# Raw expert weights fetched from slot 8 on, transposes one chunk ahead, and the row products in two halves of 64 tokens

## The chip, the cores and the metric

One core of a Trainium2 chip runs the whole program. The metric is the time of one execution on the device in microseconds (us), the median of several runs. Five engines work side by side, each through its own queue in order: TensorE (PE in the profile; its weight loads are PEld), VectorE (DVE), ScalarE (ACT), GpSimd (POOL) and SyncE (SP), which here only issues DMAs.

## What is computed

A linear attention with a decaying state, and behind it a mixture of experts with one expert per token:

```python
def _attn_ref(r, k, v, w, u):             # B, H, S, D = 4, 8, 768, 48
    state = zeros((B, H, D, D))
    for t in range(S):
        y[:, :, t] = r_t @ (state + outer(u * k_t, v_t))
        state = w_t[:, None] * state + outer(k_t, v_t)

def _moe_ref(x, w_skip, w_gate, w1, w2):  # x = y as (3072, 384), E = 8, F = 1024
    do_compute = x @ w_skip > 0           # the others keep x
    e_idx = argmax(xc @ w_gate);  gate_w = softmax(xc @ w_gate) at e_idx
    for e in range(E):
        h = maximum(xc[mask_e] @ w1[e], 0)
        out[mask_e] = xc[mask_e] + gate_w * (h @ w2[e])
```

## The kernel before

**Attention.** The 3072 tokens are 24 chunks of 128 (four sequences of six chunks; chunks 5, 11, 17 and 23 end a sequence). A loop over s (the slots, from -2 to 24) treats three chunks at a time: chunk s+2 is prepared, chunk s+1 gets its scores, and chunk s its outputs. The order of every queue is the order in which this code is written out.

- SP loads chunk s+4 (`load_chunk`: `wrk` with decays, r and k, 578 KB, and `vt` and `vN` with v) and writes the rows of a finished chunk to `out` (`store`, L479). `wrk` has three buffers, `vt` four.
- POOL makes `p` (L330), `rk` (L332) and the odd columns of r (L339) of chunk s+3, behind `kq` of chunk s+2 (L360, in `prep_keys`).
- DVE scans (`prep_scan` L344, L362), scales r to `rp` (L367), masks the scores (`mask` L396, twice a chunk) and multiplies the bonus into psY (`bonus` L408). From slot 12 on it also has the steps of the router (L248), a few of them per slot.
- PE runs per slot: `update` of the state (L418), `outputs` (L444, L450), `scores` (L380), `keys` (L389, four transposes of `kq`, copied by ACT to `kt` at L391 for the next `update`; a chunk that ends a sequence has none), `bonus_sums` (L404), and `rows_out` (L464). `quadratic(i)` at L299 writes out scores, mask, keys, bonus_sums and bonus of one chunk. `rows_out` turns the chunk's output `xT` into rows, with the router's logits beside them: four products with 128 tokens as the weights and 105 moving columns.
- ACT copies results out of the accumulators (L391, L456, L474, L478, L436).

**Experts.** Every expert has two weight matrices; each is fetched raw (3 pieces of 0.5 MB on SP, `load_weights`, L101) and split into a high part (ACT copies it to a rounded type) and a low part (raw minus high): six slices of 512 columns for each matrix. `raws[e, q]` names the raw tile of expert e: q=0 for w1 and q=1 for w2. Raw tile `r0` holds (0,0), `r1` holds (0,1), and then (1,0), and then (1,1), so each of these fetches waits until the one ahead in that tile has been split.

Two tables say when this is done in the attention: `W_AT` (fetch of (0,1) in slot 19, of (0,0) in slot 20, of (1,0) in slot 24) and `S_AT` (slices 6 to 11, that is w2 of expert 0, in slots 21 to 23, high part on ACT and low part on POOL, L710). What is left of expert 1's w1 is split in the passage behind the loop.

**The passage between.** Behind slot 24 the last router group (chunks 18 to 23) runs on DVE, while PE computes expert 0's first 128 tokens (`early_expert`, L137 and L628). Four of the six slices of (1,0) are put into the queues there (`first_split`, L733: ACT, then POOL), then the token list `idr` is made (L748), POOL gathers the second 128 tokens of expert 0 (`gather(1, None)`, L720 into `xg1`), and the last two slices follow. PE transposes these tokens (`early_tokens(1)`, L598), finishes the first ones (last four products of L628; DVE adds `fin0` at L631) and starts on the second ones (L137 again, in `expert(0)`). Then come experts 1 to 7, PE without a gap.

## Time and profile before

| | |
|---|---|
| runs | 313.95, 313.95, 315.13 us; median 313.95 |
| the profiled execution | 313.69 us, of which 311.8 us are the span from the first to the last instruction |
| attention, to the last `rows_out` | to 147.9 us of the span |
| passage to expert 1's tokens | 147.9 to 177.0 us |
| experts behind it | 177.0 to 311.8 us |
| PE busy over the span | 282.8 us (91%) |
| DVE, ACT, POOL busy | 222.8, 135.5, 161.9 us |

Times in the rows are microseconds from the span's start unless marked ns. Where a row has a start and a duration, the durations of matmuls overlap, since they are pipelined; from one group's start to the next one's is what a group costs. In brackets stands the idle time of the engine before a row and whose event ended it.

### The profile page before, as it was taken

The page shows a single profiled execution, that of the slowest core. Times are in us where ns is not written, and L with a number is a line of the kernel's source. Part 1 is how long each engine was busy: PE and PEld are TensorE (multiplying, and loading weights), DVE is VectorE, ACT ScalarE, POOL GpSimd, SP SyncE. Part 2 cuts the span into 40 slices and gives each one's busy share as a digit, 9 for nine tenths or more (in the row PEclk, how much of TensorE's full clock was granted, in tenths as well). Part 3 has the DMA queues.
Part 4 walks back from the last instruction along what each step waited for, and adds up shares of the span by engine and source line. Part 5 has one row for each costly group of instructions (what it writes and reads, how often), then busy time and mean ns, then how long its engine had stood idle before and what let it go on. Part 6 is the DMA issues. An engine that isn't in the chain of part 4 may idle for free.

```text
span 311.8 us, 8950 instructions
## 1 busy us (share of the span) xinstructions
PE 282.8 (91%) x3593; PEld 254.8 (82%) x3593; DVE 222.8 (71%) x481; ACT 135.5 (43%) x336; POOL 161.9 (52%) x155
## 2 busy tenths in 40 slices
PE   7979999999799797979935999999999999999892
PEld 2568878887687676767825999999999999999892
DVE  7789888878899996983840669586776849495320
ACT  3034334433343241335430659292957749182300
POOL 8899999897787787365493412231212223201111
PEclk9999999999999997999995899999999999999999
DMA  6999989869866868821629298969698784820001
GB/s 189 238 238 249 286 247 261 259 170 277 228 173 200 233 190 246 315 97 60 223 80 330 72 355 290 363 220 300 235 318 282 222 302 140 258 103 25 8 6 39
DMA packets 27706, 64.93 MB, mean 208 GB/s; under 512 B 4156, under 2 KB 15392, under 8 KB 27654
## 3 DMA queue, kind: packets, MB, share of 16 engines
q1 hardware_dynamic: 25350, 58.46, 61.1%
q0 software_dynamic: 2048, 5.48, 5.3%
q8 instruction: 30, 0.49, 0.7%
q10 hardware_dynamic: 256, 0.33, 0.4%
q14 instruction: 22, 0.18, 0.2%
HBM read 57.20 MB, written 7.86 MB: 209 GB/s over the span
## 4 chain that ended last, share of the span: by engine, by line
PE 70%; DVE 12%; DMA 8%; POOL 4%; issue 3%; ACT 1%; SPq 1%; POOLq 0%; DVEq 0%; ACTq 0%
PE psO L879 7%; PE psO L877 7%; PE psO L878 7%; PE psH L850 7%; PE psH L852 6%; PE psH L851 6%; PE psY L444 6%; PE psA L380 5%; DVE asb L396 4%; PE psY L450 3%; DMA vt<-wrk 3%; PE psX L464 3%; PE psY L404 3%; DVE psY L408 3%; PE psT L389 3%
## 5 line engine op out<-in xcount | busy, mean ns | idle before, releaser
L814 POOL DMA_INDIRECT out<-fin,ids x16 | 16.9, 1057 | 84.3 <-DVE fin L884 51.4
L850 PE MATMUL psH<-xTh,w1h 128*128 128x256 f32 x168 | 47.6, 284 | 0.0
L852 PE MATMUL psH<-xTh,w1l 128*128 128x256 f32 x168 | 47.5, 283 | 0.0
L851 PE MATMUL psH<-xTl,w1h 128*128 128x256 f32 x168 | 47.5, 283 | 0.0
L857 ACT ACTIVATE hh<-psH 128x256 fp32r<-128x256 f32 x60 | 23.3, 389 | 54.7 <-PE psH L852 47.9
L877 PE MATMUL psO<-w2h,hh 128*128 128x384 f32 x120 | 40.8, 340 | 0.0
L858 DVE SCALAR_TENSOR_TENSOR hl<-psH,hh 128x256 fp32r<-128x256 f32 x60 | 25.3, 421 | 21.7 <-ACT hh L857 21.4
L879 PE MATMUL psO<-w2h,hl 128*128 128x384 f32 x120 | 40.2, 335 | 0.0
L878 PE MATMUL psO<-w2l,hh 128*128 128x384 f32 x120 | 40.1, 334 | 0.0
L360 POOL TENSOR_TENSOR kq<-wrk,q 128x512 f32<-128x512 f32 x24 | 26.9, 1119 | 20.5 <-DVE q L344 13.6
L339 POOL TENSOR_TENSOR wrk<-wrk 128x512 f32<-128x512 f32 x24 | 36.1, 1506 | 2.4 <-DVE rk L332 0.6
L396 DVE TENSOR_TENSOR asb<-psA,c_sb 128x512 f32<-128x512 f32 x48 | 30.8, 684 | 8.1 <-PE psA L380 7.9
L456 ACT COPY xT<-psY 128x512 f32<-128x512 f32 x24 | 14.1, 586 | 48.8 <-PE psY L450 35.5
L852 PEld LDWEIGHTS psH<-xTh,w1l 128*128 128x128 f32 x168 | 32.2, 192 | 0.0
L850 PEld LDWEIGHTS psH<-xTh,w1h 128*128 128x128 f32 x168 | 32.2, 191 | 0.0
L851 PEld LDWEIGHTS psH<-xTl,w1h 128*128 128x128 f32 x168 | 32.2, 192 | 0.0
L444 PE MATMUL psY<-asb,vN 128*64 128x128 f32 (+1 forms) x384 | 26.6, 282 | 4.5 <-DVE psY L408 4.3
L720 POOL DMA_INDIRECT xg<-out,idr x15 | 16.2, 1078 | 27.3 <-PE psH L852 14.0
L332 POOL TENSOR_TENSOR rk<-wrk 128x512 f32<-128x512 f32 x23 | 29.5, 1283 | 0.0
L107 DVE TENSOR_TENSOR w2l<-r,w2h 128x512 fp32r<-128x512 f32 x42 | 27.8, 687 | 0.4
L884 DVE SCALAR_TENSOR_TENSOR fin<-psO,gates,xg 128x384 f32<-128x384 f32 x15 | 9.3, 618 | 25.1 <-PE psO L879 25.1
L107 DVE TENSOR_TENSOR w1l<-r,w1h 128x512 fp32r<-128x512 f32 x36 | 24.8, 689 | 1.8
(155 smaller groups left out, 653.3 us busy)
## 6 DMA issues: line engine op xcount, KB each, us to landing
r<-w SPq DMA_DIRECT2D x48, 512.0 KB, 6.4
wrk<-wrk SPq DMA_DIRECT2D x23, 577.9 KB, 6.0
wp<-wrk SPq DMA_DIRECT2D x9, 516.0 KB, 4.7
vN<-vN SPq DMA_DIRECT2D x12, 384.0 KB, 4.2
out<-x SPq DMA_DIRECT2D x24, 192.0 KB, 4.0
vt<-wrk SPq DMA_DIRECT2D x24, 96.0 KB, 3.9
vt<-wrk SPq DMA_DIRECT2D x48, 48.0 KB, 3.7
out<-fin,ids POOLq DMA_INDIRECT x16, 4.5
```

What stands on the lines that cost most here:

```text
L107: (eng or nc.vector).tensor_tensor(dst_l, src, dst_h.bitcast(F32), op=ALU.subtract)
L332: (nc.gpsimd if i else nc.vector).tensor_tensor(rk.rearrange("p a j -> p (a j)"), t[:, R_OFF:K_OFF], t[:, K_OFF:V_OFF], op=ALU.mult)
L339: nc.gpsimd.tensor_tensor(rk1, rk1, two(1, 1, CW), op=ALU.mult)
L360: nc.gpsimd.tensor_tensor(pairs(kq), pairs(wk["k"]), twice(wk["q"][:, :, 1:HW]), op=ALU.mult)
L396: nc.vector.tensor_tensor(s, psa[g], tri.rearrange("p (o j) -> p o j", o=1).to_broadcast([P, NP, P]), op=ALU.mult)
L444: nc.tensor.matmul(quarter(0, a, g, w), head(i, 2 * a + g, w), wk["asb"][g][:, a], start=False, stop=(c == 0), skip_group_check=True)
L850: nc.tensor.matmul(ps, w1h[:, o:o + P], xTh[:, kc], start=(kc == 0), stop=False)
L851: nc.tensor.matmul(ps, w1h[:, o:o + P], xTl[:, kc], start=False, stop=False)
L852: nc.tensor.matmul(ps, w1l[:, o:o + P], xTh[:, kc], start=False, stop=(kc == KC - 1))
L877: nc.tensor.matmul(pso, h[j, fc][0], w2h[:, o], start=(fc == 0), stop=False)
L878: nc.tensor.matmul(pso, h[j, fc][0], w2l[:, o], start=False, stop=False)
L879: nc.tensor.matmul(pso, h[j, fc][1], w2h[:, o], start=False, stop=(fc == FC - 1))
```

## The change

1. **Raw weights.** `W_AT` now has one piece of 0.5 MB in each of nine slots: (0,1) in slots 8, 10 and 12, (1,0) in 14, 16 and 18, and (0,0) in 19, 20 and 21. (1,0) gets a raw tile of its own, `r2`.
2. **Split.** The high parts of (0,1) and (1,0) are cast on ACT one per slot, in slots 11 to 22, behind `store`. Ten low parts go to POOL in slots 21 to 23, ahead of `evict`, and two to DVE at the end of slots 22 and 23. `S_AT` and `first_split` are gone, and so are the subtractions in the passage.
3. **Transposes.** `keys` is taken out of `quadratic` and called for chunk s+2 behind it; `bonus_sums` follows `scores` at once.
4. **Rows.** `rows_out` makes eight products of 64 tokens each where it made four of 128; the two halves of the tokens go to the two halves of the output's partitions.

```diff
-W_AT = {19: ((0, 1),), 20: ((0, 0),), 24: ((1, 0),)}
-S_AT = {21: ((0, 6), (0, 7)), 22: ((0, 8), (0, 9)), 23: ((0, 10), (0, 11))}
+W_AT = {8: (0, 1), 10: (0, 1), 12: (0, 1), 14: (1, 0), 16: (1, 0), 18: (1, 0), 19: (0, 0), 20: (0, 0),
+        21: (0, 0)}
+CASTS = [(0, i) for i in range(6, 12)] + [(1, i) for i in range(6)]
+CAST0 = 11
+LOWS = {21: CASTS[:3], 22: CASTS[3:7], 23: CASTS[7:10]}
+LOWS_V = {22: CASTS[10:11], 23: CASTS[11:]}
...
     def load_weights(e, q):
-        m = 1 if e == 1 else q
-        wr = wset0.tile([P, KC * DF], F32, tag=f"r{m}", name=f"r{m}_{e}{q}")
+        if (e, q) == (1, 0):
+            wr = third[0]
+        else:
...
+        third.append(pers.tile([P, KC * DF], F32, name="r2"))
...
             mask(i, 1)
-            keys(i)
             bonus_sums(i)
...
             for a in range(NP):
                 o = (a // 2) * X2 + (a % 2) * 2 * D
-                nc.tensor.matmul(px[:, o:o + XW], xT[:, a],
-                                 wgo_sb[:, a // 2] if a % 2 else wgp_sb[:, a], start=(a == 0),
-                                 stop=(a == NP - 1), skip_group_check=True)
+                for j in (0, HP):
+                    nc.tensor.matmul(px[j:j + HP, o:o + XW], xT[:, a, j:j + HP],
+                                     wgo_sb[:, a // 2] if a % 2 else wgp_sb[:, a],
+                                     start=(a == 0), stop=(a == NP - 1), skip_group_check=True)
...
                 if on(s - 1):
                     store(s - 1)
+                if 0 <= s - CAST0 < len(CASTS):
+                    cast(*CASTS[s - CAST0])
...
                         products(s + 3)
+                for i in LOWS.get(s, ()):
+                    low(*i, nc.gpsimd)
                 if on(s):
                     evict(s)
...
                     drip(2 * pace[0])
+                if on(s + 2):
+                    keys(s + 2)
...
+                for i in LOWS_V.get(s, ()):
+                    low(*i, nc.vector)
                 if s in W_AT:
-                    for e, q in W_AT[s]:
-                        drain(load_weights(e, q))
-                for i in S_AT.get(s, ()):
-                    split_slice(*i, nc.gpsimd)
-                    nc.gpsimd.tensor_tensor(*lows.pop(0), op=ALU.subtract)
+                    if W_AT[s] not in gens:
+                        gens[W_AT[s]] = load_weights(*W_AT[s])
+                    next(gens[W_AT[s]])
...
-                if 8 <= turn < 12:
-                    first_split()
...
             gather(1, None)
-            while firsts:
-                first_split()
             drain(load_weights(1, 1))
```

PE's queue in slot 5, from the last score of chunk 6 to the first output of chunk 6 (`psT` are the transposes, `psX` the rows, `psu` the state), before:

```order
L380 MATMUL psA1_113<-rp6_691,kq6_679 64x64
L389 MATMUL psT6_789<-c_sb_94,kq6_679 128x128 x4
L404 MATMUL psY_111<-rk6_592,ubk_sb_95 64x128 x8
L464 MATMUL psX5_805<-wgp_sb_101,xT5_764 128x105
L464 MATMUL psX5_805<-wgo_sb_102,xT5_764 128x105
L464 MATMUL psX5_805<-wgp_sb_101,xT5_764 128x105
L464 MATMUL psX5_805<-wgo_sb_102,xT5_764 128x105
L418 MATMUL psu_110<-vN1_90,kt6_794 64x48 x8
L444 MATMUL psY_111<-asb0_6_785,vN1_90 64x128
```

And after:

```order
L393 MATMUL psA1_114<-rp6_708,kq6_696 64x64
L417 MATMUL psY_112<-rk6_612,ubk_sb_96 64x128 x8
L402 MATMUL psT7_826<-c_sb_95,kq7_784 128x128 x4
L478 MATMUL psX5_833<-wgp_sb_102,xT5_792 64x105 x2
L478 MATMUL psX5_833<-wgo_sb_103,xT5_792 64x105 x2
L478 MATMUL psX5_833<-wgp_sb_102,xT5_792 64x105 x2
L478 MATMUL psX5_833<-wgo_sb_103,xT5_792 64x105 x2
L431 MATMUL psu_111<-vN1_90,kt6_745 64x48 x8
L457 MATMUL psY_112<-asb0_6_813,vN1_90 64x128
```

The bonus sums have moved ahead of the transposes, the transposes are those of chunk 7 instead of chunk 6, and the rows are eight products of 64 tokens.

POOL's queue from its last `kq` to the gathers for expert 1 (`w2l0` and `w1l1` are low parts, `xg` gathered tokens), before:

```order
L360 TENSOR_TENSOR kq23_2320<-wrk2_84,q23_2301 128x512
L587 DMA xg0_64<-out,id0_70 128x384
L710 TENSOR_TENSOR w2l0_0_2378<-r1_01_2165,w2h0_0_2377 128x512 x6
L733 TENSOR_TENSOR w1l1_1_2550<-r1_10_2501,w1h1_1_2549 128x512 x4
L720 DMA xg1_65<-out,idr_2506 128x384
L733 TENSOR_TENSOR w1l1_1_2550<-r1_10_2501,w1h1_1_2549 128x512 x2
L720 DMA xg2_2667<-out,idr_2506 128x384
```

And after:

```order
L373 TENSOR_TENSOR kq23_2429<-wrk2_84,q23_2410 128x512
L132 TENSOR_TENSOR w2l0_0_1317<-r1_01_1121,w2h0_0_1316 128x512 x3
L601 DMA xg0_64<-out,id0_70 128x384
L132 TENSOR_TENSOR w2l0_0_1317<-r1_01_1121,w2h0_0_1316 128x512 x3
L132 TENSOR_TENSOR w1l1_1_1938<-r2_91,w1h1_1_1937 128x512 x4
L740 DMA xg1_65<-out,idr_2616 128x384
L740 DMA xg2_2763<-out,idr_2616 128x384
```

Three subtractions have moved ahead of the first gather, and two of the twelve have left POOL for DVE.

SP's queue from the store of chunk 20 on (`r1_11` is the raw w2 of expert 1), before:

```order
L479 DMA out<-x20_2284 128x384
L479 DMA out<-x21_2384 128x384
L479 DMA out<-x22_2454 128x384
L479 DMA out<-x23_2491 128x384
L101 DMA r1_10_2501<-w12 128x1024 x3
```

And after:

```order
L493 DMA out<-x20_2392 128x384
L108 DMA r0_00_2273<-w12 128x1024
L493 DMA out<-x21_2488 128x384
L108 DMA r1_11_2716<-w12 128x1024 x3
L493 DMA out<-x22_2564 128x384
L493 DMA out<-x23_2605 128x384
```

The fetch of (1,0) behind the stores is gone, and that of (1,1) stands ahead of the last two stores.

## Rows read from the trace of the kernel before

**Rows 1.** The page: granted TensorE clock in 40 slices, in tenths.

```profile
PEclk9999999999999997999995899999999999999999
```

**Rows 2.** Stages: span, length, busy PE PEld DVE ACT POOL, PEclk, DMA share, GB/s.

```profile
55.30:60.50 5.20, 5.20 (x113) 4.42 (x109) 4.26 (x9) 2.04 (x7) 4.48 (x5) 1.00 0.72 192
...
103.50:110.00 6.50, 4.78 (x96) 3.93 (x92) 6.32 (x17) 1.90 (x7) 5.25 (x5) 1.00 0.81 236
...
115.40:124.90 9.50, 7.03 (x119) 6.03 (x115) 6.64 (x20) 2.52 (x9) 7.49 (x9) 0.82 0.84 261
```

**Rows 3.** PE in order of time, a full slot: start, duration, line, operation.

```profile
55.27 0.47 PE L464 MATMUL psX<-wgp_sb,xT 128*128 128x105 f32 x2
...
56.34 0.67 PE L418 MATMUL psu<-vN,kt 128*64 128x48 f32 x16
56.84 1.05 PE L444 MATMUL psY<-asb,vN 128*64 128x128 f32 x16
57.82 0.66 PE L450 MATMUL psY<-rp,sblk 64*64 64x128 f32 x16
58.30 1.05 PE L380 MATMUL psA<-rp,kq 64*64 64x64 f32 x32
59.29 0.66 PE L389 MATMUL psT<-c_sb,kq 128*128 128x128 f32 x4
59.87 0.67 PE L404 MATMUL psY<-rk,ubk_sb 64*64 64x128 f32 x16
60.47 0.36 PE L464 MATMUL psX<-wgp_sb,xT 128*128 128x105 f32 x1
```

**Rows 4.** PE in order of time, the slots around chunk 2 and slot 4.

```profile
22.93 1.05 PE L380 MATMUL psA<-rp,kq 64*64 64x64 f32 x32
...
38.58 1.05 PE L380 MATMUL psA<-rp,kq 64*64 64x64 f32 x32
39.47 0.67 PE L404 MATMUL psY<-rk,ubk_sb 64*64 64x128 f32 x16
...
41.64 1.09 PE L444 MATMUL psY<-asb,vN 128*64 128x128 f32 x16 [0.43 <-DVE psY L408]
```

**Rows 5.** POOL in order of time: kq of chunks 3 and 23.

```profile
23.84 1.12 POOL L360 TENSOR_TENSOR kq<-wrk,q 128x512 f32<-128x512 f32 x1
...
135.73 1.12 POOL L360 TENSOR_TENSOR kq<-wrk,q 128x512 f32<-128x512 f32 x1 [1.29 <-DVE q L344]
```

**Rows 6.** DMA issues: KB each, median us from issue to landing.

```profile
r<-w SPq DMA_DIRECT2D x48, 512.0 KB, 6.4
wrk<-wrk SPq DMA_DIRECT2D x23, 577.9 KB, 6.0
```

**Rows 7.** All engines in order of time in the passage behind the loop.

```profile
147.90 2.19 PE L137 MATMUL psH<-xT,r 128*128 128x128 f32 x18
...
154.97 5.99 POOL L733 TENSOR_TENSOR w1l<-r,w1h 128x512 fp32r<-128x512 f32 x4 [4.63 <-ACT w1h L118]
155.05 0.19 DVE L748 TENSOR_REDUCE idr<-psu 128x16 uint32<-128x32 f32 x1 [0.47 <-PE psu L563]
155.16 1.65 DVE L606 TENSOR_TENSOR h0l<-hf,h0h 128x512 fp32r<-128x512 f32 x1
...
157.22 0.45 PE L628 MATMUL psO<-w2h,h0h 128*128 128x384 f32 x1 [1.05 <-ACT h0h L617]
...
158.72 0.86 PE L628 MATMUL psO<-w2h,h0l 128*128 128x384 f32 x4
...
161.11 1.02 POOL L720 DMA_INDIRECT xg<-out,idr  x1 [0.15 <-issue]
...
166.25 0.88 PE L598 MATMUL psX<-c_sb,xg 128*128 128x128 f32 x3 [6.67 <-DMA xg<-out,idr]
...
169.21 7.81 PE L137 MATMUL psH<-xT,r 128*128 128x128 f32 x48 [0.80 <-DVE fin L631]
```

**Rows 8.** Granted clock in the passage, columns as in rows 2.

```profile
169.00:171.00 2.00, 1.79 (x8) 1.82 (x9) 0.07 (x1) 0.00 (x0) 0.00 (x0) 0.50 1.03 423
```

More of the change, by code (lines that the diff above doesn't have):

```diff
@@ L727, in rwkv_moe_kernel @@
         gates = keep.tile([P, 2, E], F32, name="gates")
[L728 to L733 removed]
         with tc.manual_schedule():
[L736 removed]
+            todo, due, done = early_expert(), HEAD * STEP, [0]
             while later:
```

28 lines of the change are left out of this document (13 added, 15 removed).

## The prediction, made before the changed kernel ran

> **What bounds the kernel now.** I read the stages first (granted clock and busy time of each engine), then PE's queue in order of time, then who waits for whom. Three regions come out, and the experts behind them, which the change doesn't touch: there PE runs without a gap in both.
>
> *Slots 1 to 12* are PE's. A slot without router work takes 5.20 us, and PE is busy for 5.20 of it, while DVE has 4.26 and POOL 4.48 [rows 2]. PE's queue shows what fills it [rows 3]: rows 1.07 (55.27 to 56.34), update 0.50, outputs 0.98 + 0.48, scores 0.99, transposes 0.58, bonus sums 0.60. A microsecond taken from PE there is taken from the end, until DVE or POOL is next.
>
> *Slots 13 to 21* are DVE's: it has the router as well. In the stage from 103.5 to 110.0 DVE works 6.32 of 6.50 us and PE 4.78 [rows 2]. There PE's savings are mostly idle time for PE. From 115.4 to 124.9 neither is full; the granted clock is 0.82 in the mean, since PE sat idle ahead of it [rows 2].
>
> *The passage from 147.9 to 177.0* belongs to one chain: DVE finishes the token list at 155.24, but the gather that needs it is issued at 161.11, because POOL has four subtractions (154.97 to 160.96) ahead of it; the tokens land at 166.25, and PE has waited 6.67 us for them [rows 7]. [...]
>
> **The change part by part.** The sum is made against the profiled execution, 313.69 us, 0.26 below the median of 313.95; the 0.26 is added at the end.
>
> *The passage: 7.8 us.* The subtractions of (1,0) are made in slots 21 to 23, so nothing stands in POOL's queue between the token list and the gather. POOL's last `kq`, of chunk 23, ends at 136.85 [rows 5]; ten subtractions at 1.50 (5.99 for four [rows 7]) and a gather at 1.02 [rows 7] make 16.0, so POOL is through at 152.9, ahead of 155.24. The gather then goes out 0.15 behind the list, at 155.4, and lands 5.14 later as now (161.11 to 166.25), at 160.5: 5.7 us earlier. ACT's four casts go too, which held `h0h` back until PE had waited 1.05 for it [rows 7]; PE is then out of work at 158.7 + 0.86 - 1.05 = 158.5 and idle for 2.0 instead of 6.67. What comes behind the landing took 2.96 (166.25 to 169.21) and 7.81 (48 instructions of L137) at partly half clock. At full clock 18 such instructions took 2.19 [rows 7], so 48 take 5.84, and the 2.96 fall to about 2.1 (an estimate: DVE's and ACT's part stays, PE's halves). At full clock the whole is 5.7 + 0.9 + 2.0 = 8.6; if PE's clock falls in the 2.0 us gap, 5.7. A gap of that length lies between two that the trace shows: from 103.5 to 110.0 PE is idle for 1.72 us in all (6.50 - 4.78) and the clock stays at 1.00; from 115.4 to 124.9 it is idle for 2.47, and the mean falls to 0.82 [rows 2]. I take 7.8, nearer to the full clock.
>
> *Rows in two halves: 0.30 us per chunk where PE sets the pace.* The trace of before has no 105-column product with 64 weights; the nearest rows have the same form (all 128 rows of the array, half its columns). Eight outputs of 128 columns take 0.98, eight updates of 48 columns 0.50 [rows 3]. A straight line between gives 0.84 for 105 columns, 0.23 under today's 1.07. The two ends, 0.98 and 0.50, bound the saving by 0.09 and 0.57. Then there is a cost whenever the form changes: scores followed by transposes take 0.99 (58.30 to 59.29), scores followed by bonus sums, which have their form, 0.89 (38.58 to 39.47) [rows 3, 4]: 0.10. A slot has four such changes now around transposes and rows, and two after, because the bonus sums follow the scores and the rows have the update's form. Part of that is inside the 1.07 already; I take 0.07, and 0.30 in all.
>
> [...]
>
> *What that is worth in slots 1 to 12: 2.8 us.* Eleven slots at 0.30 are 3.3. Against it stands a wait of PE for DVE. From the start of the bonus sums to the outputs DVE needs 2.17 (39.47 to 41.64) for masks and bonus [rows 4]. Today only the slot without transposes and update is shorter (1.67; a wait of about 0.43). Now the missing transposes and the missing update fall into neighbouring slots: 0.60 + 0.77 + 0.50 = 1.87 and 0.60 + 0.58 + 0.77 = 1.95, two waits of 0.3 and 0.2 for one of 0.4, which is nothing gained or lost. The transposes one chunk ahead need `kq` of the same slot. For chunk 3 it ends at 24.96 [rows 5]; PE would be there at 22.93 + 0.89 + 0.60 = 24.42 [rows 4]: 0.5 lost, once. Later POOL's own work, 4.48 a slot [rows 2], stays below PE's 4.90. So 3.3 - 0.5 = 2.8; with the bounds of the rows, 0.5 to 5.
>
> *Slots 13 to 21: 0.6.* DVE's work stays. One slot there is PE's (0.3). The dip of the clock at 119 depends on when PE falls idle; PE idles somewhat longer than now, so it may vanish (2.3 us of DVE's 2.9 idle in that stage [rows 2]) or a second may come. I take another 0.3 from it; bounds -2.5 to +2.5.
>
> *Slots 22 and 23: 0.4.* The last rows save 0.3, and the router's copy no longer stands behind a cast on ACT (0.1).
>
> *Raw pieces from slot 8 on: nothing.* Nine DMAs of 512 KB move, with the load of the next chunk behind each in SP's queue. In slot 8 the DMA engines are busy for 0.72 of 5.20 us, at 192 GB/s; the fullest rate of a stage in these rows is 423 GB/s [rows 2, 8]. A piece costs 1.2 us of all engines at that rate and 2.7 at the former; every other slot has one, so 0.6 to 1.4 a slot, on 3.7. That is 4.3 or 5.1 against a slot of 4.9: hidden, or 0.2 a slot too much. I take the first, since 192 GB/s is the rate of a stage that was not full; the second would be some 1 us in slots 8 to 12. The load of `wrk` lands 6.0 after issue [rows 6], so 7 to 9 behind a piece; its buffer comes free about two slots ahead of its use, 9.8 us. The cover is thin, and without it a piece costs its 1.2 to 2.7. In slots 19 and 20 there is less than now (six pieces then, two now).
>
> *Casts on ACT, subtractions on DVE: nothing.* ACT is busy for 2.04 of 5.20 [rows 2]; a cast stands behind `store`, while PE runs update and outputs (1.96 from 56.34 to 58.30 [rows 3]), and only then has ACT the next copy to make. Uncovered it would be some 0.6 in each of twelve slots. The two subtractions on DVE may take 1.65 beside POOL, as `h0l` did [rows 7]; they stand at the ends of slots 22 and 23, where DVE has no chunk left to prepare. The gather of expert 0's first tokens now stands behind three subtractions on POOL, 4.5 at 1.50; its tokens are wanted only behind the outputs of chunk 23, at about 146. POOL issues it at 136.85 + 4.5 = 141.4; landing in 5.14 like the later one, it would be there at 146.5, so up to 0.5 late. The fetch of (1,1) waits on SP for the sixth subtraction, with the last two stores behind it: 136.85 + 1.02 + 6 times 1.50 = 146.9, ahead of the last rows, which end at 147.9 [rows 7].
>
> Sum: 7.8 + 2.8 + 0.6 + 0.4 = 11.6; 313.69 - 11.6 + 0.26 = 302.3 us.
>
> **Rivals.**
> 1. *Only the passage gains.* The rows cost 0.98 and the new waits take the rest: 7.8 + 0.5, 305.7. Or with the clock lost in the passage as well, 5.7 + 0.5: 307.8. For it: DVE and POOL stand at 4.3 and 4.5 in a slot of 5.2 [rows 2]. Against: a whole slot still has 0.4 between them and PE.
> 2. *The clock holds everywhere.* 8.6 in the passage, 2.3 more at 119, 4 in slots 1 to 12: 16, or 298. For it: half-clock stretches are due to gaps, and the largest shrinks.
> 3. *The raw pieces crowd out the chunk loads: slower.* In slots 8 to 21 a piece that isn't hidden keeps POOL waiting for `wrk`, and all behind it. Nine pieces at 2.7 are 24; less the 11.6 above that is 326. It turns slower once a piece costs over 1.3 us of the chain. Against: 0.28 of the DMA time is free in slot 8.
> 4. *The halves run one after the other.* Then rows take 8 times 0.27 = 2.14, PE's slot 6.27; eleven slots give +11.8, and nine of DVE's slots +0.6 each: 313.95 + 17.2 - 7.8 = 323. It decides from 1.07 + 0.6 per chunk on. Against: the outputs' 0.98.
> 5. *The subtractions or the stores behind the fetch are late*, so that the gather goes out as late as now: 313.95 - 2.8 - 0.6 - 0.4 = 310.2. POOL has 2.3 us in hand for this.
>
> **Chances.** Forecast, within about 2 us: 0.55. Rival 1: 0.17. Rival 2: 0.12. Rival 5: 0.06. Rivals 3 and 4: 0.05 and 0.02; in milder form (a few pieces unhidden) rival 3 ends near no change, 0.03. A measurement here can tell about 0.5% from no change, 1.6 us. Faster by more: 0.90; within: 0.04; slower: 0.06. The range runs from 298, where rival 2 ends, to 308, where rival 1 does; it leaves out rivals 3 to 5.
>
> **What the profile after would show.** The gather for the second tokens within 0.5 us of the token list, no subtraction of POOL between them, and PE's idle time ahead of L598's second transposes at 2 us instead of 6.67. PE's group of rows at about 0.85, and a full slot of 4.9. Granted clock in the passage: 1.00, or a dip of one stretch. Wrong would be: POOL's `p` waiting for DMA in slots 9 to 20 (rival 3), rows over 1.1 (rival 4), new idle time of PE ahead of the transposes, with POOL's `kq` as releaser (rival 1), or the passage's gather behind a store that lands late (rival 5).

## The result, and the profile after

The changed kernel takes 309.34 us (median of 4 runs, 309.07 to 310.79) against 314.38 of the kernel before on the same chip (median of 4, 313.95 to 315.13). The ratio is 0.985, 95% interval 0.981 to 0.989: faster by 5.0 us, where 11.6 had been forecast, and outside the range of 298 to 308. A ratio leaves out the runs that lie over 1.5% above the fastest of their kernel; a median does not.

The two profiled executions (spans 311.8 and 309.0 us) split as follows. The marks are starts of PE's work: the rows of chunks 1, 12 and 23, and the token transposes of expert 1. The columns are the time up to the first mark, then from mark to mark, then the rest. The table is worked out from the traces; the same is done for every experiment below, where the last columns are the median time and that of the kernel before in the same comparison. The comparisons ran on several chips, so a time is to be read against its own time before. The last column but one is a single run for e5, e7, e13, e14 and e15, and a median of 4 to 10 for the others.

```
kernel               start  1->12  12->23  passage   rest    span    time  before
before               25.10  55.09   66.73    29.94  134.94  311.8  314.38
after                27.22  51.26   70.53    24.50  135.49  309.0  309.34  314.38
difference           +2.12  -3.83   +3.80    -5.44   +0.55   -2.8
forecast              0     -2.8    -1.0     -7.8     0
e1_lows_pool         26.91  52.17   67.79    19.48  135.35  301.7  304.60  315.27
e2_piece_later       27.37  52.79   66.89    25.89  135.16  308.1  310.95  315.27
e3_keys_back         24.99  53.48   67.56    22.21  134.96  303.2  309.24  315.27
e4_rows_whole        27.08  56.79   66.19    25.64  135.60  311.3  312.94  315.27
e5_rows_only         25.66  53.20   66.91    30.04  135.59  311.4  313.21  314.75
e6_late_pieces       27.09  51.73   66.53    19.32  135.33  300.0  301.48  314.75
e7_pieces_alone      25.20  55.27   65.09    29.68  134.86  310.1  311.99  314.75
e8_late_hybrid       26.38  53.34   65.75    19.44  135.29  300.2  302.00  314.75
e9_pieces_back       27.27  52.46   65.96    21.01  135.50  302.2  304.01  315.70
e10_late_whole       26.70  52.02   66.17    23.61  135.20  303.7  306.72  315.70
e11_late_keys_back   26.07  53.53   68.08    19.31  135.61  302.6  303.02  315.70
e12_whole_fetch      27.66  51.84   65.68    19.63  135.09  299.9  301.88  314.23
e13_double           27.41  57.19   66.51    19.50  135.49  306.1  307.84  312.57
e14_double_before    27.07  55.32   67.73    30.82  135.06  316.0  317.90  312.57
e15_again            28.48  52.31   64.20    24.24  135.27  304.5  306.31  312.57
```

So the rows and the transposes brought what was forecast in slots 1 to 12, and more; the start and the slots behind 12 lost 5.9 us that no term of the sum had; and the passage gave 2.4 less.

The page of the changed kernel, granted clock and DMA share in 40 slices (the first answers [rows 1]):

```profile
PEclk9979999999979997899979999999999999999999
DMA  6999999999986789641706399969697876710001
```

There are four dips in the clock instead of two, but the long one of the passage is short now. Stages of the changed kernel (columns as in [rows 2]: the first answers the slot of 5.20 there, the second lies where PE stops, the third where the clock stays at half longest):

```profile
53.00:60.00 7.00, 7.00 (x174) 5.81 (x166) 5.80 (x12) 2.95 (x9) 6.84 (x7) 1.00 0.92 237
83.00:92.00 9.00, 5.98 (x119) 5.31 (x113) 4.64 (x12) 2.66 (x7) 4.36 (x5) 0.84 0.91 241
119.00:127.00 8.00, 6.14 (x103) 5.74 (x103) 5.08 (x16) 1.50 (x5) 5.97 (x7) 0.57 0.97 283
```

In the first POOL is busy for 6.84 of 7.00: it is full beside PE now, where it had 4.48 of 5.20 [rows 2].

PE in a slot of the changed kernel (start, duration, line, operation; it answers [rows 3]):

```profile
54.41 0.66 PE L402 MATMUL psT<-c_sb,kq 128*128 128x128 f32 x4
54.99 0.40 PE L478 MATMUL psX<-wgp_sb,xT 128*64 128x105 f32 x4
55.22 0.35 PE L478 MATMUL psX<-wgo_sb,xT 128*64 128x105 f32 x4
...
55.76 0.62 PE L431 MATMUL psu<-vN,kt 128*64 128x48 f32 x16
```

From rows to update are 0.77 us instead of 1.07. That is near the price that the prediction's straight line had found (0.84), and two halves cost nowhere near the 2.14 of its fourth rival (twice the 1.07 of [rows 3]).

The start: PE waits for POOL's `kq` of chunk 1, whose transposes now stand ahead of chunk 0's update and outputs. Then its clock is at half (0.50 from 17.4 to 20.8):

```profile
15.75 0.66 PE L402 MATMUL psT<-c_sb,kq 128*128 128x128 f32 x4 [2.08 <-POOL kq L373]
16.33 0.67 PE L431 MATMUL psu<-vN,kt 128*64 128x48 f32 x16
16.83 1.41 PE L457 MATMUL psY<-asb,vN 128*64 128x128 f32 x16
18.18 1.75 PE L393 MATMUL psA<-rp,kq 64*64 64x128 f32 x29
```

In slot 13 PE stops between the second and the third of four transposes, for 3.02 us. The view names "issue": nothing that it shows was being waited for.

```profile
85.16 0.44 PE L402 MATMUL psT<-c_sb,kq 128*128 128x128 f32 x2
88.61 0.38 PE L402 MATMUL psT<-c_sb,kq 128*128 128x128 f32 x2 [3.02 <-issue]
```

The passage, DVE, POOL and PE in order of time (it answers [rows 7]):

```profile
146.47 6.76 DVE L132 TENSOR_TENSOR w1l<-r,w1h 128x512 fp32r<-128x512 f32 x1
...
153.47 0.67 DVE L132 TENSOR_TENSOR w1l<-r,w1h 128x512 fp32r<-128x512 f32 x1
154.06 0.25 DVE L262 TENSOR_REDUCE lg<-lgs 128x54 f32<-128x108 f32 x1
...
161.96 0.19 DVE L758 TENSOR_REDUCE idr<-psu 128x16 uint32<-128x32 f32 x1 [1.74 <-PE psu L577]
144.05 3.74 POOL L132 TENSOR_TENSOR w2l<-r,w2h 128x512 fp32r<-128x512 f32 x3
147.74 4.94 POOL L132 TENSOR_TENSOR w1l<-r,w1h 128x512 fp32r<-128x512 f32 x4
162.43 1.22 POOL L740 DMA_INDIRECT xg<-out,idr  x1 [9.75 <-DVE idr L758]
...
155.86 0.18 PE L525 MATMUL psu<-oh,trib 128*128 128x48 bf16 x1 [3.70 <-DVE psu L262]
...
156.04 5.22 PE L150 MATMUL psH<-xT,r 128*128 128x128 f32 x30
...
166.06 0.52 PE L612 MATMUL psX<-c_sb,xg 128*128 128x128 f32 x3 [0.89 <-DMA xg<-out,idr]
...
168.08 5.59 PE L150 MATMUL psH<-xT,r 128*128 128x128 f32 x48 [0.80 <-DVE fin L645]
```

The gather did follow the list at once (162.43 behind 162.15), and PE waits 0.89 for the tokens instead of 6.67. But the list itself is late. One of the two subtractions on DVE takes 6.76 us. The router's first step stands behind it, PE waits 3.70 for the router, and its clock falls to half behind that wait (0.50 from 157.3 to 160.7): thirty instructions of L150 take 5.22, where forty-eight take 5.59 later on.

### The profile page after: what moved, and what is told of

It reads as the page before. It is cut to its first block, busy times and chain, and to the rows that moved or that the text cites. A ratio compares the mean times of both kernels' runs of the same rounds, so it can differ in the third digit from the quotient of the medians.

```text
span 309.0 us, 9345 instructions
## 1 busy us (share of the span) xinstructions
PE 277.0 (90%) x3785; PEld 252.1 (82%) x3785; DVE 226.5 (73%) x483; ACT 135.9 (44%) x336; POOL 159.0 (51%) x153
## 4 chain that ended last, share of the span: by engine, by line
PE 59%; DVE 15%; DMA 12%; POOL 8%; issue 3%; ACT 1%; SPq 0%; POOLq 0%; DVEq 0%; ACTq 0%
DMA vt<-wrk 7%; PE psO L885 7%; PE psO L887 7%; PE psO L886 7%; PE psH L858 7%; PE psH L860 7%; PE psH L859 7%; DVE asb L409 4%; PE psY L457 4%; PE psH L150 3%; DVE psY L421 3%; DVE w1l L132 2%; PE psY L463 2%; DMA wgp_sb<-wgp 2%; PE psA L393 2%
## 5 line engine op out<-in xcount | busy, mean ns | idle before, releaser
L457 PE MATMUL psY<-asb,vN 128*64 128x128 f32 (+1 forms) x384 | 27.9, 290 | 4.4 <-DVE psY L421 4.3
L393 PE MATMUL psA<-rp,kq 64*64 64x128 f32 (+1 forms) x768 | 27.3, 261 | 0.0
```

The source lines that it names most:

```text
L393: nc.tensor.matmul(psa[g][j:j + HP, a, j:], wk["kq"][rows, a, j:j + HP], wk["rp"][rows, a, j:], start=True, stop=True)
L457: nc.tensor.matmul(quarter(0, a, g, w), head(i, 2 * a + g, w), wk["asb"][g][:, a], start=False, stop=(c == 0), skip_group_check=True)
```

## The experiments

### The subtraction on DVE

The two DVE subtractions go to POOL, behind its ten others.

```
-LOWS = {21: CASTS[:3], 22: CASTS[3:7], 23: CASTS[7:10]}
-LOWS_V = {22: CASTS[10:11], 23: CASTS[11:]}
+LOWS = {21: CASTS[:3], 22: CASTS[3:7], 23: CASTS[7:]}
+LOWS_V = {}
```

> The changed kernel with all twelve subtractions on POOL, none on DVE. Theory A (in the changed kernel one DVE subtraction took 6.76 us, 146.47 to 153.23, since POOL's subtractions ran back to back until 152.68, and the router's list waited for it): the last two stores' copies stay where they are, the reduction that opens the last router part goes out at about 150.4 instead of 154.06, the token list is 3.6 us earlier, POOL has two more subtractions of 1.25 each and is through at 155.2, ahead of the list at 158.3; PE waits about 0.1 instead of 3.70 for its rank products, perhaps without the half clock behind it (1.7 more). Time 304 to 306. Rival: the list waits for something else at the same place (the store of the last scores, 150.00 to 150.4, or the weights' fetch); then the time stays within 1 us of 309.3.

304.60 us, ratio to before 0.968 (0.959 to 0.976). The passage takes 19.48 instead of 24.50. Its rows:

```profile
148.06 0.27 DVE L262 TENSOR_REDUCE lg<-lgs 128x54 f32<-128x108 f32 x1 [3.36 <-ACT lgs L488]
...
145.60 7.42 POOL L132 TENSOR_TENSOR w1l<-r,w1h 128x512 fp32r<-128x512 f32 x6
155.19 1.22 POOL L740 DMA_INDIRECT xg<-out,idr  x1 [2.17 <-DVE idr L758]
```

DVE is idle until the copy of the last scores arrives, the list follows, and POOL has been idle for 2.17 when it can gather. The clock stays full through the whole passage. Theory A holds. In the changed kernel the long subtraction ended 0.55 us behind the last of POOL's seven (153.23 against 147.74 + 4.94 = 152.68), and the next one, with POOL idle, took 0.67. Four more executions have this subtraction on DVE, unchanged. It took 6.78 in e2_piece_later, e4_rows_whole and e15_again and 5.58 in e3_keys_back, where one subtraction fewer of POOL's was left, and each time it ended 0.55 behind POOL's last. In e3_keys_back:

```profile
143.50 5.58 DVE L132 TENSOR_TENSOR w1l<-r,w1h 128x512 fp32r<-128x512 f32 x1
```

### PE's stops without a named releaser

The trace records the DMA packets of a queue of instructions (q8; in the changed kernel 32 packets, each of 16 KB), one every 4 to 14 us in the loop; that they are PE's is read from the count below. Over all executions of this study PE stopped 22 times with no named releaser; each stop ended 1.25 to 1.72 us behind the landing of such a block. These are the ones that the text speaks of:

```
execution        block landed   PE goes on   behind it   PE had stopped for
after                   87.18        88.61        1.43                 3.02
e1_lows_pool            66.31        67.78        1.47                 1.03
e1_lows_pool            87.98        89.23        1.25                 1.62
e2_piece_later          86.57        87.98        1.41                 1.38
e4_rows_whole           79.92        81.48        1.56                 3.86
e6_late_pieces          50.01        51.73        1.72                 0.60
e8_late_hybrid          50.86        52.45        1.59                 1.97
e9_pieces_back          67.02        68.43        1.41                 1.12
e12_whole_fetch        111.78       113.44        1.66                 0.89
e13_double              67.96        69.54        1.58                 1.37
e13_double              75.70        77.10        1.40                 1.92
```

That points to PE having run out of instructions, and a count shows the same. In PE's records (products, weight loads and the semaphore instructions among them, from the start of the program) every one of the 22 stops comes 193 or 194 behind a whole multiple of 256 (3265 ahead of the stop of 3.02, which is 12 times 256 and 193), and that multiple is the number of blocks that had landed when PE went on (12, the last at 87.18). So what PE had done kept step with what had landed, and each stop is the end of the block before. These places are fixed by the program; the one in slot 13 is the same in the first execution of the changed kernel, e1_lows_pool, e2_piece_later, e3_keys_back and e15_again, with stops of 3.02, 1.62, 1.38, 0.75 and 0.83 us. What makes a block late? First, one raw piece moved:

```
-W_AT = {8: (0, 1), 10: (0, 1), 12: (0, 1), 14: (1, 0), 16: (1, 0), ...
+W_AT = {8: (0, 1), 10: (0, 1), 14: (0, 1), 15: (1, 0), 16: (1, 0), ...
```

> The changed kernel with one raw piece moved from slot 12 to slot 14 (and the next from 14 to 15). Theory B: PE stopped for 3.02 us within one chunk's four transposes (85.6 to 88.6) with no wait that the profile names, because its own instruction block of 16 KB landed late: blocks came every 5 to 7 us, this one 10.4 us behind the last (75.73, then 86.10 to 87.25), while the DMA engines were busy for the whole stretch (share 1.03 to 1.07 from 60 to 85 us) behind a raw piece issued at 78.51 and a chunk load at 79.10. With that piece gone from there, the block comes 6 to 7 us behind the last, the stop is under 0.5 us, the half clock at 89.1 to 92.5 (1.7 us) is gone, and the time falls by 3 to 4.5, to 305 to 306.5. Rival: the stop belongs to the number of instructions at that place, whatever the DMA engines do; then it stays at 3 us and the time within 0.5 of 309.3. A further possibility: the stop moves to another slot, which would speak for theory B with another place.

The stop in slot 13 fell from 3.02 to 1.38 and the half clock behind it went: slots 12 to 23 took 66.89 instead of 70.53. The time did not follow (310.95 us, ratio to before 0.984, 0.979 to 0.989), since slots 1 to 12 took 1.5 more and the passage 1.4 more, the latter with twice the time at half clock (3.4 us in the changed kernel). A miss for the time, half an answer for the cause.

Then all pieces late, with all subtractions on POOL as in the first experiment:

```
+W_AT = {14: (0, 1), 15: (0, 1), 16: (0, 1), 17: (1, 0), 18: (1, 0), 19: (1, 0), 20: (0, 0), 21: (0, 0),
+        22: (0, 0)}
+CAST0 = 18        (and two casts a slot from there)
```

> All twelve subtractions on POOL as in the first experiment, and the raw pieces one a slot in slots 14 to 22 instead of 8 to 21, with two casts a slot on ACT in slots 18 to 23. Theory B (PE's instruction blocks land late where raw pieces fill the DMA engines in slots 8 to 13; each unexplained stop of PE ended 1.25 to 1.56 us after a block had landed): no stop of PE without a named releaser in slots 8 to 13; slot 13 takes 7 to 7.5 us instead of 10.4; 2.5 to 3.5 us less than the first experiment's 303.4 to 305.1, so 300 to 302. Cost against it: casts in pairs delay ACT's copies by up to 0.6 a slot in six slots, up to 2 us. Rival (the stops come from the order of PE's instructions alone): slot 13 still takes 10 us, time 304 to 306.

301.48 us, ratio to before 0.958 (0.951 to 0.965), 3.1 under e1_lows_pool, whose interval overlaps (0.959 to 0.976); the two profiled executions are 1.7 apart. No stop in slots 8 to 13; slot 13 took 7.26. There is one of 0.60 in slot 7, where no raw piece has been loaded yet. Next, only the first three pieces back, with the casts left late:

```
-W_AT = {14: (0, 1), 15: (0, 1), 16: (0, 1), 17: (1, 0), ...
+W_AT = {8: (0, 1), 10: (0, 1), 12: (0, 1), 17: (1, 0), ...
```

> The kernel of e6_late_pieces with only the first three raw pieces moved back to slots 8, 10 and 12; the casts stay late, so that only the DMAs differ. In e6_late_pieces PE had no stop without a named releaser in slots 8 to 13, and slot 13 took 7.26 us. Theory B (a block of PE's instructions waits behind the bytes already in the DMA queues): a stop of 0.5 to 3 us comes back in slots 8 to 14, 1.2 to 1.6 us behind a block that lands 9 to 11 us after the last; time 1 to 3 us over e6_late_pieces, 302 to 304.5. Rival (in the first version of the change it was ACT's casts from slot 11 on, or chance): no stop there, slot 13 at 7.3, time within 0.7 of 301.5.

304.01 us. A stop of 1.12 came back, in slot 10, though its block landed 7.3 us behind the last and not 9 to 11. ACT's casts have no part in it. The time fell into the expected range for another reason: of the 2.2 us between the two profiled executions 1.7 lie in the passage, where the clock was at half for 3.4 us here and full in e6_late_pieces. The other way round, the same three pieces in the kernel before:

```
+P_AT = (8, 10, 12)
+                if s in P_AT:
+                    if s == P_AT[0]:
+                        gens[0] = load_weights(0, 1)
+                    next(gens[0])
```

> The kernel before with one thing moved: the three raw pieces of the first 1.5 MB load in slots 8, 10 and 12 instead of all behind slot 19. Theory B: the DMA engines come to a share near 1 in slots 8 to 13, one block of PE's instructions arrives over 8 us behind the last, and PE stops for 0.5 to 3 us with no named releaser somewhere in slots 8 to 14. Weaker form: PE uses up its instructions more slowly here (5.03 us a slot instead of 4.66, and eight products fewer in it), so the blocks are just in time and the stop stays under 0.5 us. Rival (the stops belong to the changed order): none at all, with blocks 8 us and more apart.

No stop at all, with a DMA share of 1.01 at 284 GB/s from 60 to 85 us; 311.99 us. Bytes alone didn't do it here. Last, twice the bytes in both orders (these two load the three pieces in slots 8 to 10, and the same three a second time in slots 11 to 13), and the changed kernel once more:

```
+                if s in (11, 12, 13):
+                    o = (s - 11) * 1024
+                    nc.sync.dma_start(raws[0, 1][:, o:o + 1024],
+                                      w12[0, :, KC * DF + o:KC * DF + o + 1024])
```

> The kernel of e9_pieces_back with the first three raw pieces in slots 8 to 10 and the same three loaded once more in slots 11 to 13: twice the bytes, nothing else added. Theory B (blocks wait behind bytes in the DMA queues): PE's stops without a named releaser in slots 8 to 15 add up to 2 to 6 us (1.1 in e9_pieces_back, 0 in e6_late_pieces), each ending 1.2 to 1.6 us behind a block; besides, chunk loads may land late and POOL's p wait for them. Rival (the stops are a matter of phase, and bytes have no part): 0 to 1.1 us as before.

> The kernel before with the same six loads in slots 8 to 13 (three pieces, each twice). In the kernel before with three of them in slots 8, 10 and 12 PE had no such stop, with blocks 7.6 and 7.8 us after the last. Theory B in its plain form: with twice the bytes the old order stops too, 0.5 to 4 us in slots 8 to 15. Theory B with PE's pace (the old order uses up its instructions more slowly: 5.03 us a slot instead of 4.66, and the whole rows are eight instructions fewer): under 0.5 us, while e13_double stops for 2 or more.

> The changed kernel once more, nothing changed. If the stop belongs to a place in the program, it comes again in slot 13 (as in the first execution and in e1_lows_pool and e2_piece_later, which differ little from it): 1.4 to 3 us behind a block that comes 8 to 10.5 us after the last, with time 308.5 to 311. If it is chance, it is in another slot or missing, and the time 305.5 to 311.

PE's stops in e13_double:

```profile
69.54 0.31 PE L463 MATMUL psY<-rp,sblk 64*48 64x128 f32 x1 [1.37 <-issue]
77.10 0.32 PE L393 MATMUL psA<-rp,kq 64*64 64x128 f32 x3 [1.92 <-issue]
```

Together 3.29 us, against 1.12 with half the bytes and none in those slots without; slots 1 to 12 grew by 4.7 over e9_pieces_back, 1.7 of it by a half clock of 3.4 us behind the second stop. In e14_double_before there was none. The stretch from 60 to 85 us, columns as in [rows 2], of before, e14_double_before, the changed kernel, e6_late_pieces, e9_pieces_back and e13_double in turn:

```profile
60.00:85.00 25.00, 23.00 (x469) 19.38 (x470) 21.41 (x46) 8.69 (x26) 19.66 (x18) 1.00 0.83 239
```

```profile
60.00:85.00 25.00, 23.27 (x478) 19.58 (x471) 20.95 (x42) 9.66 (x29) 21.04 (x19) 1.00 1.03 280
```

```profile
60.00:85.00 25.00, 22.76 (x554) 19.67 (x553) 22.22 (x49) 11.35 (x32) 21.88 (x21) 1.00 1.05 285
```

```profile
60.00:85.00 25.00, 22.75 (x547) 19.52 (x549) 22.22 (x50) 9.81 (x29) 21.35 (x21) 1.00 0.93 249
```

```profile
60.00:85.00 25.00, 21.66 (x509) 18.30 (x509) 21.06 (x45) 9.13 (x27) 20.66 (x19) 1.00 1.02 290
```

```profile
60.00:85.00 25.00, 21.30 (x450) 17.68 (x442) 17.69 (x36) 7.71 (x23) 17.58 (x17) 0.93 1.02 267
```

The DMA share (last but one) in this stretch is 0.94 to 1.05 in all kernels that load raw pieces there, in either order, and 0.83 to 0.93 in those that don't. PE's instructions in it (products alone), where it doesn't stop, are 533 to 554 with the halves, 495 and 506 with whole rows and the transposes ahead, and 469 to 478 in the old order. Over the whole study, PE's stops in slots 8 to 15 add up to 1.1 to 3.9 us in each of the eight executions with raw pieces in slots 8 to 13 and PE's work changed (halves, transposes or both); to 0.2 at most in the six with PE's work changed and no piece before slot 14; and to nothing in the two with the old order and pieces. So in these slots it took both: full queues, and an order that uses instructions up faster. The late pieces show the same in one order: from 88 to 120 us the queues of e6_late_pieces are as full, but DVE sets the pace there, PE gets through 18 of them a us instead of 22 (19 in the old order), and it doesn't stop:

```profile
88.00:120.00 32.00, 26.07 (x587) 22.27 (x583) 30.38 (x76) 12.04 (x33) 24.25 (x22) 0.94 1.03 279
```

That a block waits behind bytes already in the queues fits all of this, but the trace doesn't show when a block was asked for, so that last link is argued, not shown. The stops in slot 7 of e6_late_pieces and e8_late_hybrid, and one of 0.97 in slot 2 of e11_late_keys_back, came where only the chunks' own loads were under way; there too the share was 0.99 to 1.00 between the landing of the block before and that of the late one. So raw pieces are one way to fill the queues, not the only one.

e15_again stopped four times in slots 12 to 16, 4.0 us in all, and nowhere for 3 us:

```profile
80.79 0.40 PE L478 MATMUL psX<-wgp_sb,xT 128*64 128x105 f32 x4 [1.33 <-issue]
87.33 0.38 PE L402 MATMUL psT<-c_sb,kq 128*128 128x128 f32 x2 [0.83 <-issue]
94.25 0.31 PE L478 MATMUL psX<-wgp_sb,xT 128*64 128x105 f32 x2 [1.18 <-issue]
99.93 0.38 PE L431 MATMUL psu<-vN,kt 128*64 128x48 f32 x6 [0.67 <-issue]
```

The kernel took 306.31 all the same (312.57 before, on that chip), since its clock was full from slot 14 to the passage (from 88 to 150 us, e15_again and then the first execution of the changed kernel):

```profile
88.00:150.00 62.00, 49.91 (x1127) 42.19 (x1124) 55.46 (x126) 24.00 (x66) 48.23 (x44) 1.00 0.76 221
```

```profile
88.00:150.00 62.00, 52.27 (x1114) 44.66 (x1114) 51.05 (x121) 23.65 (x64) 44.04 (x40) 0.92 0.64 186
```

Which of the fixed places a stop hits, and what it costs in clock, differs from execution to execution; 3 and 4 us of stops were in the two.

### The transposes one chunk ahead

```
             mask(i, 1)
+            keys(i)
             bonus_sums(i)
...
-                if on(s + 2):
-                    keys(s + 2)
```

> The changed kernel with the transposes put back between scores and bonus sums of their own chunk. Theory C: the transposes ahead cost 2.1 us in the first slots (PE waits 2.08 for POOL's kq of chunk 1 ahead of chunk 0's outputs, and 1.7 are lost at half clock), and save only form changes of 0.1 a slot afterwards, about 1.1 in slots 1 to 12; the rows of chunk 1 then start at about 25.1 instead of 27.2, those of chunk 12 1.0 earlier than now, and the time falls by about 1, to 308.3, if nothing behind absorbs it. Rival: the early loss comes from the raw pieces or the rows in halves, neither of which is undone here; then the rows of chunk 1 stay at 27.2, and the time rises by about 1.

The rows of chunk 1 start at 24.99, as before the change: the 2.1 us at the start belong to the transposes ahead. Of these, 0.6 are the transposes of chunk 3, which stand ahead of this mark now and come behind it in the old order, so they are moved and not lost. From there to the rows of chunk 11 are 49.07, of which 0.85 are a stop, so 48.2, against 46.65 in the changed kernel. The time is that of the changed kernel (309.24, ratio to before 0.985, 0.977 to 0.994).

Two kernels on the base of e6_late_pieces: the first three chunks' transposes in the old place, or all of them.

```
e8:   if on(s + 2) and s >= 1: keys(s + 2)    and in quadratic: if i < 3: keys(i)
e11:  keys(i) in quadratic for all chunks, as in e3_keys_back
```

> The kernel of e6_late_pieces with the transposes of the first three chunks at their old place, ahead only from chunk 3 on. Theory C: PE doesn't wait for chunk 1's kq ahead of chunk 0's outputs, and its clock stays full there, so the rows of chunk 1 start at 25.0 (25.10 before, 24.99 with all transposes back) instead of 27.2: 2 us less than e6_late_pieces, 298 to 300. Rival: DVE and POOL, which set the pace behind, take the 2 us back by slot 12; then within 0.7 of e6_late_pieces.

> The kernel of e6_late_pieces with all transposes back between scores and bonus sums of their own chunk. From runs so far: the rows of chunk 1 start 1.5 to 2 us earlier (25.0 to 25.7 instead of 27.09), ten chunks take 47.6 to 48.2 instead of 46.5, so by chunk 11 the two are about even, within 0.8. Behind it DVE sets the pace in both. Theory C/E: time within 1.2 us of e6_late_pieces. Rival (the transposes ahead are what brought the gain, 0.3 a slot in all 22 slots): 3 us slower.

302.00 and 303.02 us against 301.48. In e8_late_hybrid the rows of chunk 1 started at 26.38, with chunk 3's transposes (0.6) ahead of them as in e6_late_pieces (27.09), so 0.7 were saved at the start and not 2; a stop of 1.97 in slot 7, where e6_late_pieces has 0.60, took them back. That run tells nothing of DVE and POOL taking them. In e11_late_keys_back the rows of chunk 1 started at 26.07 and the ten chunks took 49.11, 1.2 of them stops. Its time agrees with that of e6_late_pieces within the scatter of the runs (300.11 to 304.38 and 300.54 to 303.51; both ratios 0.958).

### The rows in two halves

```
-                for j in (0, HP):
-                    nc.tensor.matmul(px[j:j + HP, o:o + XW], xT[:, a, j:j + HP], ...
+                nc.tensor.matmul(px[:, o:o + XW], xT[:, a], ...
```

> The changed kernel with the rows as one product of 128 tokens. Theory D: the halves are worth 0.30 us a chunk (1.07 to 0.77 from rows to update) wherever PE sets the pace, so slots 1 to 12 grow by 3.3 and the time to about 312, a little less if waits for POOL's kq, which the halves opened, close again. Rival: the halves only turn PE's time into waits for DVE and POOL; then slots 1 to 12 stay within 1 us of their 51.26 and the time within 1 of 309.3.

312.94 us (ratio to before 0.986, 0.975 to 0.998), as theory D has it, but not for the reason given. Ten chunks (rows 1 to 11) took 47.22, only 0.57 more than with the halves. The runs scatter from 308.37 to 315.75, and the profiled one (313.21) had the longest stop of the study, in the middle of slot 12:

```profile
76.75 0.87 PE L393 MATMUL psA<-rp,kq 64*64 64x128 f32 x21
81.48 0.70 PE L393 MATMUL psA<-rp,kq 64*64 64x64 f32 x11 [3.86 <-issue]
```

The halves alone in the kernel before:

> The kernel before with the rows in two halves and nothing else. From the rows of chunk 1 to those of chunk 11 the kernel before takes 50.33 us. Theory D (the prediction's): 0.30 a chunk where PE sets the pace, so 47.3 to 47.6. Theory E (POOL, with 4.5 us of work a chunk, and DVE are next in line, so the two savings of PE don't add: transposes ahead alone, with whole rows, took 47.22, both together 46.65): here the halves stand alone and find room, 47.6 to 48.0, with two or three more waits of PE for DVE's bonus than before. Rival: under 1 us saved, since the rows' cost turns into waits. The passage stays as before (29 us); time about 311 on a quiet chip.

Ten chunks took 48.79, of which 0.81 are a wait of chunk 2's update for a load of `vN`; without it 48.0, against 50.33 before. So each of the two edits alone brings 2.3 to 3.1 us in ten chunks, and both together 3.7: they don't add. On the base of e6_late_pieces:

> The kernel of e6_late_pieces with the rows as one product. Theory E (once the transposes are ahead, DVE's and POOL's work sets most of a slot, and the halves are worth only about 0.06 to 0.10 us a chunk: 46.65 against 47.22 from the rows of chunk 1 to those of chunk 11 in the changed kernel with and without them): 47.0 to 47.4 for the ten chunks, time 0.5 to 1.5 over e6_late_pieces, 302 to 303. Theory D (0.30 a chunk wherever PE sets the pace): 49.5, time 304.5. By theory B in its wider form (the halves' eight further PE instructions a chunk bring the next block's due time nearer) the small stop in slot 7 (0.6 us) also goes, so that the whole rows lose even less.

47.40 for the ten chunks, as theory E has it, and no stop at all. The rows of chunk 23 even start 0.46 earlier than in e6_late_pieces (144.89). In a slot with whole rows and the transposes ahead, rows to update take 0.97, not 1.07:

```profile
60.07 0.37 PE L477 MATMUL psX<-wgp_sb,xT 128*128 128x105 f32 x2
...
61.04 0.67 PE L431 MATMUL psu<-vN,kt 128*64 128x48 f32 x16
```

But 306.72 us (ratio to before 0.970, 0.959 to 0.981) are 3.7 over the expectation, and all of it lies in the passage. PE waits 3.53 for tokens that were gathered late (and works at half clock for 3.4 us behind that):

```profile
152.94 0.19 DVE L758 TENSOR_REDUCE idr<-psu 128x16 uint32<-128x32 f32 x1 [0.47 <-PE psu L576]
...
154.44 1.32 POOL L740 DMA_INDIRECT xg<-out,idr  x1 [3.42 <-DVE ids L766]
...
159.64 0.52 PE L611 MATMUL psX<-c_sb,xg 128*128 128x128 f32 x3 [3.53 <-DMA xg<-out,idr]
```

The view names DVE's `ids`, which this gather does not read. It reads what the stores have written, and the last packet of a store ended at 153.23, behind the list, because the 1.5 MB of expert 1's second half stood ahead of the last two stores on SP. So that fetch was put behind them, by making it depend on ACT's last copy:

```
-            drain(load_weights(1, 1))
+            drain(load_weights(1, 1, copied[-1]))
```

> The kernel of e10_late_whole (whole rows, late pieces, all subtractions on POOL) with the fetch of expert 1's second half put behind the last two stores on SP instead of ahead of them. In e10_late_whole the gather went out 1.31 us behind the end of the token list (154.44 against 153.13; 0.28 in the kernels with halves), and the last packet of a store ended at 153.23; its passage took 23.6 us against 19.3, though the rows of chunk 23 started 0.46 earlier (144.89 against 145.35). Theory F (the prediction's fifth rival in a small form: the stores, behind 1.5 MB of fetch, landed last): the gather goes out within 0.3 of the list, its tokens land 3.5 to 3.8 behind, PE waits about 0.8 instead of 3.53, and the passage takes 19.3 to 20; time 299.5 to 301.5, so the whole rows cost nothing against the halves of e6_late_pieces (theory E). Rival: the gather was late for another reason, passage still over 22, time 303.5 to 306; or the fetch, 2 us later now, makes expert 1's split late and gives back up to 2 us behind the passage.

301.88 us; the last store's packet ends at 148.46, the gather goes out 0.27 behind the list, and PE waits 0.9 again:

```profile
153.22 0.19 DVE L762 TENSOR_REDUCE idr<-psu 128x16 uint32<-128x32 f32 x1 [0.48 <-PE psu L580]
...
153.68 1.22 POOL L744 DMA_INDIRECT xg<-out,idr  x1 [2.37 <-DVE idr L762]
```

With that, whole rows and halved rows stand at the same time (301.88 and 301.48; ratios 0.963 and 0.958, with intervals that overlap): once the transposes are ahead, the halves are worth nothing that can be measured here. By e11_late_keys_back the reverse holds too: with the halves, the transposes ahead are worth nothing that can be measured. What the same kernel would take with neither was not run. e6_late_pieces and e12_whole_fetch beat both kernels.

## Why the prediction was wrong

*The passage, -7.8: the mechanism was right, one step was mis-sized.* The gather left POOL's queue free and followed the list, as said. The failed step is "the two subtractions on DVE may take 1.65 beside POOL, as `h0l` did". That row [rows 7] is of a subtraction that met four of POOL's as well, and got in behind the first of them. These are the first two, in the kernel before:

```profile
154.97 1.29 POOL L733 TENSOR_TENSOR w1l<-r,w1h 128x512 fp32r<-128x512 f32 x1 [4.63 <-ACT w1h L118]
156.22 1.73 POOL L733 TENSOR_TENSOR w1l<-r,w1h 128x512 fp32r<-128x512 f32 x1
```

`h0l` ended at 156.81 (155.16 + 1.65), 0.55 behind the first (156.26), and POOL's second took longer for it. In e5_rows_only and e14_double_before it got in the same way (1.78 and 1.80). I took its 1.65 as the price of any such meeting. Here DVE's subtraction started at 146.47, with one of POOL's under way and five behind it, and was done 0.55 behind the last of them, in 6.76; none of POOL's took over 1.28. Why it got in there and not here, no run shows. I also let it end the slot, "where DVE has no chunk left to prepare", and overlooked that the router's list, the very chain that the edit was to shorten, was next in DVE's queue. Without it (e1_lows_pool) the passage gained 10.5, more than my 8.6 at full clock: the tokens landed 3.7 behind the gather instead of 5.14 (155.19 to 158.90), and the granted clock was full all through, where the kernel before has 0.50 [rows 8].

*Slots 1 to 12, -2.8: measured -3.8.* The price of the halves was right (0.77 where 0.84 was estimated). The attribution was not. I gave the transposes ahead a part of 0.07 a slot and called their waits even; alone they bring 0.31 a chunk (50.33 to 47.22 over ten, e4_rows_whole), since scores, transposes and rows each take some 0.10 less beside their new neighbours: in e10_late_whole 0.89, 0.49 and 0.97, where the kernel before has 0.99, 0.58 and 1.07. The halves then add only 0.06, because POOL and DVE are next (6.84 and 5.80 of 7.00). That is the first rival's mechanism (its sign, PE's waits for POOL's `kq` ahead of the transposes, adds up to 3.5 us in the changed kernel, 2.1 of them at the start), but it set in behind the gain and not in place of it. The fourth rival, the halves one after the other, is refuted: eight half-wide products from start to start take 0.77.

*The start, 0: measured +2.1, of which 0.6 are the moved transposes of chunk 3.* I had looked for the wait for `kq` at chunk 3 (0.5) and not at chunk 1, where POOL is still busy with the first products (`p`, `rk` and the odd columns of r from 11.06 on, then this `kq` to 15.69). The order alone showed it: transposes of chunk 1 ahead of update and outputs of chunk 0. e3_keys_back settles it.

*Slots 13 to 23, -1.0: measured +3.8, outside the bounds of 2.5.* 3.0 are the stop. Behind it PE works at half clock for 3.4 us (0.50 from 89.1 to 92.5), which costs half of that by estimate, and the dip around slot 19 is twice as long as before (6.8 instead of 3.4). In e6_late_pieces, which doesn't stop there, the stretch takes 66.53, 0.2 less than before, with the long dip (6.8) in it: the 0.6 and 0.4 were small and stayed small.

*Raw pieces, 0 (at most 1): cost about 3 (e6_late_pieces against e1_lows_pool, 1.7 by the profiled executions).* The step that failed is the rate. I priced a piece at 423 GB/s, 1.2 us of all engines, and took the slot as covered at 4.3 of 4.9. With the pieces there the DMA engines are full (share 1.05) at 285 GB/s, so by estimate a piece costs 1.8 of all engines (0.52 MB). A chunk's own loads cost more than the 3.7 that I had: slot 8 was a light one, and from 60 to 85 us, five slots, the share before was 0.83, so 4.2 a slot. With 0.9 for half a piece that makes 5.1, on a slot that takes 4.7 in the changed kernel. No room was left, and the kernel before showed that much. The third rival had the full queues, but looked for their victim among the chunk loads, which were hidden (POOL's waits for `wrk` were 1.9 us in all); the victim was PE's own instructions, in no term and no rival. Nothing in the kernel before shows such a stop.

*The rest.* Casts on ACT cost nothing that shows, as said: behind the first rows PE's waits for ACT in the changed kernel are 0.4 us in all. The terms of the second rival add up to 14.9 and not to 16, so the lower end of the range should have been 299. The fifth rival, stores behind the fetch, did not decide the changed kernel, whose list was later still, but it was next in line: in e10_late_whole it cost some 4 us, with the clock.

The forecast's 302.3 is nearly what e6_late_pieces measures (301.5), without the two costs that I had priced at nothing. That it is so near is in part luck: the passage gains 10.6 there instead of 7.8, and slots 1 to 12 gain 3.4 instead of 2.8, which pays for 2.0 at the start, 0.8 missing behind slot 12 and 0.4 in the rest.

## What to carry to other kernels

Price a DVE operation beside a run of POOL operations by the length of the run (6.76 us here for a subtraction that took 0.67 alone), unless the trace shows that it gets in between (1.65 in the kernel before), and ask what stands behind it in DVE's queue. When PE's work is made denser while transfers are moved in beside it, count the bytes in the queues against the rate that full queues have shown (285 GB/s here, at a share of 1.05), and look for stops without a releaser: PE's own instructions come in DMA packets too (32 of 16 KB here). Two edits that both shorten one engine's slot add up only as far as the next engine leaves room (3.1 and 2.3 us alone here, 3.7 together), so each should be run alone.

## What the runs showed of the hardware that I had not expected

- A DVE subtraction of 128x512 took 0.67 us with POOL idle (the changed kernel), and 5.58 to 6.78 us in five executions where POOL ran its subtractions back to back; each time it ended 0.55 us behind the last of them. In three executions of the old passage another one got in behind POOL's first, in 1.65 to 1.80 us.
- PE stopped 22 times in twelve executions with no named releaser, for 0.2 to 3.9 us, by the count of its records each time out of instructions; each time it went on 1.25 to 1.72 us behind the landing of a 16 KB block, 193 or 194 records past a multiple of 256.
- A change of form between products cost PE some 0.10 us: rows to update take 1.07 behind bonus sums (64*64, the kernel before), and 0.97 behind transposes, which have the rows' form (128*128, e10_late_whole).
